# A decode kernel whose VectorE instructions leave the hardware loop and are written out in line

## The chip, the cores and the metric

The kernel runs on one core of one Trainium2 chip. The time is the device time of one execution in microseconds; "before" stands for the median of three runs. A profile is one further execution, recorded by the hardware profiler.

## The reference

One token (x, 1024 wide) goes through an attention block with a long cache and, beside it, through a small MLP mixer. Cut to what matters:

```python
xn = layernorm(x)
# A: attention, 32 query heads, 4 key/value heads, 65536 cached positions of 128
q = (layernorm-ed x @ wq) -> 32 heads of 128
scores = q . k_cache * 128 ** -0.5
o = softmax(scores) @ v_cache
A = o @ wo
# B: mixer
h  = gelu(layernorm(xn) @ w1)
x1 = xn + shifted(h) @ w2
B  = x1 + gelu(layernorm(x1) @ w3) @ w4
out = x + A + B
```

K and V together are 128 MiB of bfloat16, each element of which is used once; wq, wo and the four MLP weights are another 34 MiB.

## The kernel before

The kernel is written without a scheduler. Each engine has a recorder (class `_Q`, line 14): `wait`, `op` and `dma` append to a list of operations, and what an operation must wait for is worked out from buffers that note who wrote and read them last (`_deps`, line 119). At the end (lines 700 to 704) each list is emitted to its engine. `emit` (line 64) writes the list out in line. `emit_looped` (line 67) needs marks in the list: it checks that the stretches between marks have the same shape, and that every semaphore value grows by the same step from stretch to stretch, then emits one stretch as the body of a hardware loop. In the loop a wait's value is computed by register instructions (line 56, `i * steps[k] + ...`), and the loop ends in a register operation, a compare and a branch (line 93). Before the change VectorE (`q_dve`) and TensorE (`q_pe`) are emitted as loops; SyncE, ScalarE and GpSimd are written out.

The attention is 32 tiles (`NT`): 4 heads of 8 tiles, a tile being 8192 positions. The loop at line 584 records the tiles; every fourth tile is a mark, so that a loop body holds 4 tiles and runs 8 times. For tile n:

- `Ttr` (line 484): VectorE transposes K in 4 pieces of 128x1024 (L490) from the load buffer into a second buffer. The pieces of tile n+1 stand between the steps of tile n. They are what frees a K buffer.
- `QK` (line 493): 16 matmuls of PE into `S_ps` (L500).
- `stats1`, `MB`, `stats2`: the row maximum on VectorE (L509), its spread (L510), a small matmul (L515) and a reduction (L519).
- `EXP` (line 522): the running bound on VectorE (L528), ScalarE's exponential (L530), the change of the bound on VectorE (L532) and its exponential (L534).
- `PTr` and `PV` (lines 536 and 542): the weights are transposed by PE (L538) and VectorE (L540), then 16 matmuls with V (L548). They are what frees a V buffer.
- `FLASH` (line 553): ScalarE copies the result out (L556), GpSimd scales and adds it (L558 to L561).

SyncE issues all the large loads in one queue. K and V come in loads of 4 MiB, two tiles each, into two buffers of each kind; the load two steps ahead is recorded after the tile that frees its buffer (line 603). Weights follow in the same queue: w1 and w2 after tile 28, w3 after tile 30 (L323 by way of `load_at`), wo and the first 16 of w4's 28 row groups after tile 31 (channel `w40`, landing in a buffer that is not used before), and three further parts of w4 (`w41` to `w43`) once w1 and w2 have been read.

Behind the tiles come the mixer (lines 618 to 643), the merging of the heads (667 to 677), w3 (679), and the last products, in an order written by hand: wo, then w4's first two parts by `half_rows` (L660, in pairs of matmuls, 64 for wo and 44 for w4), a copy by VectorE (L689), w4's third part by `out_rows` (L452), the fold of the copy (L691), w4's fourth part, the last copy (L696) and the store of the output.

Ahead of the tiles, VectorE has 42 operations of layer norms, constants and the query, then the 4 transposes of tile 0.

Of the kernel before, what the change touches and what calls it, by code (L numbers as in the profile page):

```python
# [172 lines left out]
def bass_parallel_sum__gqa_block_cached__mixer_s_mlp__decode_kernel(  # L173
# [31 lines left out]
    with ExitStack() as es:  # L205
# [8 lines left out]
        def sem(name):  # L214
            return E(nc.semaphore(name))
# [68 lines left out]
        q_pe = _Q("pe", sem("c_pe"), in_order=True)  # L284
        q_dve = _Q("dve", sem("c_dve"))
# [152 lines left out]
        def head_switch(h):  # L438

            _deps(q_pool, [b_Y], [b_Yc])  # L440
            src = Yall[:, (h - 1) % HKV, :, :, :]
            q_pool.ops.append((2, lambda e: e.tensor_copy(Ycur[:, :, :, :], src), s_y, 2))
            for b in (b_brun[1],):
                for s, v in list(b.w.items()) + list(b.r.items()):
                    q_pool.wait((s, v))
            q_pool.ops.append((2, lambda e: e.memset(brun[:, 1:2], BIG), s_b, 2))
# [37 lines left out]
        def Ttr(n, idx):  # L484

            s, half, xs = (n // 2) % 2, n % 2, n % 2
            for ix in idx:
                c = KOFF[s] // 2 + 4096 * half + 1024 * ix
                x = (XOFF + 8192 * xs) // 2 + 1024 * ix
                _op(q_dve, lambda e, c=c, x=x: e.transpose(out=KV32[:, x:x + 1024], in_=KV32[:, c:c + 1024]),  # L490
                    reads=[b_K[s][half]], writes=[b_X[xs][ix]])

        def QK(n):
            xs = n % 2
            fns = []
            for we in range(4):
                w_hi, e_ = divmod(we, 2)
                for cm in range(4):
                    mv = bass.AP(KV[:].tensor, XOFF + xs * 8192 + cm * 128 + w_hi * 64 + e_, [[kstep, P], [512, 16], [2, 32]])
                    fns.append(lambda e, we=we, cm=cm, mv=mv: e.matmul(  # L500
                        S_ps[32 * cm:32 * cm + 32, :], Ycur[:, we, :, :].rearrange("p a g -> p (a g)"), mv,
                        start=(we == 0), stop=(we == 3), tile_position=(0, 32 * cm)))
            if n % 4 == 0:
                q_pe.wait((s_y, n // 4 + 1))
            b_Yc.add_read(_grp(q_pe, fns, reads=b_X[xs], writes=[b_S]))

        def stats1(n):
            m = n % 2
            _op(q_dve, lambda e: e.reduce_max(mrow[:, m:m + 1], S_ps[:, :], axis=AX.X), reads=[b_S], writes=[b_mrow[m]])  # L509
            _op(q_dve, lambda e: e.tensor_tensor(out=Rm[:, m, :], in0=sel16[:, :], in1=mrow[:, m:m + 1].broadcast_to([P, 16]), op=ALU.mult),  # L510
                reads=[b_mrow[m], b_const], writes=[b_R[m]])

        def MB(n):
            m = n % 2
            _op(q_pe, lambda e: e.matmul(MB_ps[:, 0:16], Lmat[:, :], Rm[:, m, :], start=True, stop=True),  # L515
                reads=[b_R[m], b_const], writes=[b_MB])

        def stats2(n):
            _op(q_dve, lambda e: e.tensor_reduce(out=Bst[:, n % 4:n % 4 + 1], in_=MB_ps[:, 0:16], axis=AX.X, op=ALU.min),  # L519
                reads=[b_MB], writes=[b_Bcol[n % 4]])  # L520

        def EXP(n):
            m = n % 2
            ko = 1 - m
            cL = 513 * m
            if n % 4 == 0:
                q_dve.wait((s_b, n // 4 + 1))
            _op(q_dve, lambda e: e.tensor_tensor(out=brun[:, m:m + 1], in0=brun[:, ko:ko + 1], in1=Bst[:, n % 4:n % 4 + 1], op=ALU.min),  # L528
                reads=[b_brun[ko], b_Bcol[n % 4]], writes=[b_brun[m]])
            _op(q_act, lambda e: e.activation(p_sb[:, m, :], S_ps[:, :], ACTF.Exp, bias=brun[:, m:m + 1], scale=SCALE, accum_out=tmpO[:, cL:cL + 1]),  # L530
                reads=[b_S, b_brun[m]], writes=[b_p[m], b_tmpL[m]])
            _op(q_dve, lambda e: e.tensor_tensor(out=dd[:, m:m + 1], in0=brun[:, m:m + 1], in1=brun[:, ko:ko + 1], op=ALU.subtract),  # L532
                reads=[b_brun[ko], b_brun[m]], writes=[b_dd[m]])
            _op(q_act, lambda e: e.activation(ff[:, m:m + 1], dd[:, m:m + 1], ACTF.Exp), reads=[b_dd[m]], writes=[b_ff[m]])  # L534

        def PTr(n):
            m = n % 2
            _op(q_pe, lambda e: e.matmul(PT_ps[:, :], permR[:, :], p_sb[:, m, :], start=True, stop=True),  # L538
                reads=[b_p[m], b_const], writes=[b_PT])
            _op(q_dve, lambda e: e.transpose(out=pT_f[:, :], in_=PT_ps[:, :]), reads=[b_PT], writes=[b_pT])  # L540

        def PV(n):
            s = (n // 2) % 2
            v0 = VOFF[s] + 8192 * (n % 2)
            fns = []
            for q in range(16):
                q4 = q % 4
                fns.append(lambda e, q=q, q4=q4: e.matmul(OT_ps[32 * q4:32 * q4 + 32, :], pT_bf[:, q, :, 1],  # L548
                                                          KV[:, v0 + 512 * q:v0 + 512 * (q + 1)],
                                                          start=(q < 4), stop=(q >= 12), tile_position=(0, 32 * q4)))  # L550
            _grp(q_pe, fns, reads=[b_pT, b_V[s]], writes=[b_OT])

        def FLASH(n):

            m = n % 2
            _op(q_act, lambda e: e.activation(tmpO[:, 1:513], OT_ps[:, :], ACTF.Copy), reads=[b_OT], writes=[b_tmpO])  # L556
            _deps(q_pool, [b_ff[m]], [b_Oacc])
            q_pool.op(lambda e: e.tensor_tensor(out=spare[:, 4:5], in0=ff[:, m:m + 1], in1=ff[:, m:m + 1], op=ALU.add), False)  # L558
            b_Oacc.set_write(q_pool.op(lambda e: e.tensor_scalar(out=O_acc[:, :], in0=O_acc[:, :], scalar1=ff[:, m:m + 1], scalar2=0.0, op0=ALU.mult, op1=ALU.add)))  # L559
            _deps(q_pool, [b_tmpO, b_tmpL[m], b_Oacc], [])  # L560
            ev = q_pool.op(lambda e: e.tensor_tensor(out=O_acc[:, m:m + 513], in0=O_acc[:, m:m + 513], in1=tmpO[:, m:m + 513], op=ALU.add), tick=(s_fl, n + 5))  # L561
            _done(ev, [b_ff[m], b_tmpO, b_tmpL[m]], [b_Oacc])
# [15 lines left out]
        def load_at(c0, bufs, ch, w, r0, nrow):  # L578
            load_rows(KV[:, c0:c0 + nrow * w.shape[1]], bufs, ch, w, r0, nrow)
# [3 lines left out]
        const_sems = (q_pool.sem,)  # L583
        for n in range(NT):
            if n % 4 == 0:
                q_pe.mark(const_sems)
                q_dve.mark(const_sems)
            QK(n)
            Ttr(n + 1, [0])
            stats1(n)  # L590
            MB(n)
            stats2(n)
            EXP(n)
            Ttr(n + 1, [1])
            PTr(n)
            Ttr(n + 1, [2, 3])
            if n % NSUB == NSUB - 1:
                head_switch(n // NSUB + 1)
            PV(n)
            FLASH(n)  # L600
            if n % NSUB == NSUB - 1:
                head_end(n // NSUB)
            (issue_v if n % 2 else issue_k)(n // 2 + 2)
            if n == NT - 4:
                load_at(KOFF[0], b_K[0][:1], "k0", B_w1, 0, 8)
                load_at(KOFF[0] + 8192, b_K[0][1:], "w2", B_w2, 0, 8)
            if n == NT - 2:
                b_w3 = b_K[1] + [b_V[0]]
                load_at(VOFF[0], b_w3, "w3", B_w3, 0, 8)
            if n == NT - 1:  # L610
                b_wo = [b_V[1]] + b_X[0] + b_X[1]
                load_at(VOFF[1], b_wo[:1], "wo0", A_wo, 0, 16)
                load_at(XOFF, b_wo[1:], "wo1", A_wo, 16, 16)
                load_at(WOFF, [b_W], "w40", B_w4, 0, 16)
        for q in (q_pe, q_dve):
            q.mark(const_sems)

        _grp(q_pe, [lambda e, j=j, q=q: e.matmul(M0_ps[32 * q:32 * q + 32, :], xn2_bf[:, j:j + 1].broadcast_to([P, 32]),
                                                 KV[:, j * D + 512 * q:j * D + 512 * (q + 1)],
# [80 lines left out]
        q_sp.emit(nc.sync)  # L700
        q_act.emit(nc.scalar)
        q_pool.emit(nc.gpsimd)
        q_dve.emit_looped(nc, nc.vector)
        q_pe.emit_looped(nc, nc.tensor)


# [26 lines left out]
```

## Time and profile before

| | |
|---|---|
| median of 3 runs | 403.39 us (403.23 to 403.68) |
| profiled execution, its own time | 403.03 us |
| its span, first to last instruction | 401.7 us |
| mean granted TensorE clock | 0.63 |
| busy: PE, PE weight loads, VectorE | 183.4, 53.0, 238.8 us |
| busy: ScalarE, GpSimd | 49.7, 91.9 us |
| read from HBM | 169.87 MB, 423 GB/s over the span |
| transposes of K on VectorE (L490) | 132, 156.4 us busy, 1216 ns each |
| maxima on VectorE (L509), transposes of the weights (L540) | 32 of 675 ns, 32 of 713 ns |
| instructions in VectorE's program: before, after | 168, 469 |

A busy time is the sum of an engine's operations; register, branch and wait instructions are not counted in it. A wait is put down to what ended last before the waiting operation started. The DMA row of the page gives, for 40 equal slices of the span, the busy share of the core's 16 DMA engines in tenths. The trace further holds each DMA packet with queue, start, duration and size, and the events by which a load reports: 16 for each load.

### The profile page before, as it was taken

The page shows a single profiled execution, that of the slowest core. Times are in us where ns is not written, and L with a number is a line of the kernel's source. Part 1 is how long each engine was busy: PE and PEld are TensorE (multiplying, and loading weights), DVE is VectorE, ACT ScalarE, POOL GpSimd, SP SyncE. Part 2 cuts the span into 40 slices and gives each one's busy share as a digit, 9 for nine tenths or more (in the row PEclk, how much of TensorE's full clock was granted, in tenths as well). Part 3 has the DMA queues.
Part 4 walks back from the last instruction along what each step waited for, and adds up shares of the span by engine and source line. Part 5 has one row for each costly group of instructions (what it writes and reads, how often), then busy time and mean ns, then how long its engine had stood idle before and what let it go on. Part 6 is the DMA issues. An engine that isn't in the chain of part 4 may idle for free.

```text
span 401.7 us, 4258 instructions
## 1 busy us (share of the span) xinstructions
PE 183.4 (46%) x1428; PEld 53.0 (13%) x1428; DVE 238.8 (59%) x403; ACT 49.7 (12%) x132; POOL 91.9 (23%) x173
## 2 busy tenths in 40 slices
PE   0044245563545444443444443545453636636457
PEld 0022111110111111110111111111010101213112
DVE  0024788767575758585767585858585858664201
ACT  1000021211111111111112021111111112100000
POOL 6000022231315222222432221216222222430000
PEclk9997565555655556557565565565565565575988
DMA  9989999999999999999999999999999999999995
GB/s 392 444 365 441 444 417 418 457 423 425 434 437 431 422 437 431 431 424 450 424 431 431 437 431 424 434 434 428 424 454 421 431 424 427 456 410 424 429 419 212
DMA packets 6209, 169.98 MB, mean 423 GB/s; under 512 B 820, under 2 KB 824, under 8 KB 952
## 3 DMA queue, kind: packets, MB, share of 16 engines
q1 hardware_dynamic: 6056, 169.87, 98.5%
q8 instruction: 4, 0.07, 0.1%
q14 instruction: 5, 0.04, 0.0%
q10 hardware_dynamic: 144, 0.00, 0.0%
HBM read 169.87 MB, written 0.00 MB: 423 GB/s over the span
## 4 chain that ended last, share of the span: by engine, by line
DMA 56%; DVE 19%; issue 11%; PE 11%; ACT 1%; POOL 0%; DVEq 0%; SPq 0%; ACTq 0%; POOLq 0%
DMA KV<-in_A_k_cache_dram 40%; DVE KV L490 12%; DMA KV<-in_B_w_dram 10%; DMA x_bf<-in_A_x_dram 6%; PE S_ps L500 5%; DVE mrow L509 3%; PE PT_ps L538 2%; PE S_ps L660 2%; ACT p_sb L530 1%; PE MB_ps L515 1%; DVE Rm L510 1%; DVE Bst L519 1%; DVE brun L528 1%; DVE pT_f L540 1%; PE OT_ps L548 0%
## 5 line engine op out<-in xcount | busy, mean ns | idle before, releaser
L490 DVE STREAM_TRANSPOSE KV<-KV 128x1024 f32<-128x1024 f32 x132 | 156.4, 1216 | 52.8 <-DMA KV<-in_A_k_cache_dram 52.8
L548 PE MATMUL OT_ps<-KV,pT_f 128*32 128x512 bf16 x512 | 60.7, 627 | 26.6 <-DVE pT_f L540 26.6
L500 PE MATMUL S_ps<-KV,Ycur 128*32 128x512 bf16 x512 | 58.7, 606 | 16.9 <-DVE KV L490 16.9
L561 POOL TENSOR_TENSOR O_acc<-O_acc,tmpO 128x513 f32<-128x513 f32 x32 | 41.0, 1281 | 96.4 <-ACT tmpO L556 96.4
L530 ACT ACTIVATE p_sb<-S_ps,brun 128x512 bf16<-128x512 f32 x32 | 22.0, 687 | 162.4 <-DVE brun L528 162.4
L515 PE MATMUL MB_ps<-Rm,Lmat 128*128 128x16 bf16 x32 | 6.2, 192 | 74.6 <-DVE Rm L510 74.6
L538 PE MATMUL PT_ps<-p_sb,permR 128*128 128x512 bf16 x32 | 18.3, 571 | 45.9 <-ACT p_sb L530 45.9
L556 ACT ACTIVATE tmpO<-OT_ps 128x512 f32<-128x512 f32 x32 | 19.2, 599 | 106.1 <-PE OT_ps L548 106.1
L558 POOL TENSOR_TENSOR spare<-ff 128x1 f32<-128x1 f32 x32 | 6.2, 193 | 110.9 <-ACT ff L534 110.9
L509 DVE TENSOR_REDUCE mrow<-S_ps 128x1 f32<-128x512 f32 x32 | 21.6, 675 | 16.1 <-PE S_ps L500 16.1
L540 DVE STREAM_TRANSPOSE pT_f<-PT_ps 128x512 f32<-128x512 f32 x32 | 22.8, 713 | 2.9
L500 PEld LDWEIGHTS S_ps<-KV,Ycur 128*32 128x32 bf16 x512 | 14.7, 125 | 62.1 <-issue 32.4
L548 PEld LDWEIGHTS OT_ps<-KV,pT_f 128*32 128x32 bf16 x512 | 14.7, 129 | 58.6 <-DVE pT_f L540 30.7
L559 POOL TENSOR_SCALAR O_acc<-O_acc,ff 128x514 f32<-128x514 f32 x32 | 22.4, 700 | 0.0
L515 PEld LDWEIGHTS MB_ps<-Rm,Lmat 128*128 128x128 bf16 x32 | 3.3, 102 | 101.6 <-DVE Rm L510 101.6
L689 DVE COPY KV<-S_ps 64x512 f32<-64x512 f32 x1 | 0.7, 683 | 22.7 <-PE S_ps L660 22.7
L381 PE MATMUL MM_ps<-ln_s,ones_f 128*128 128x1 f32 x6 | 1.8, 362 | 27.2 <-DVE ln_s L380 27.2
L377 DVE CAST xT<-x_bf 128x8 f32<-128x8 bf16 x1 | 0.2, 171 | 21.5 <-DMA x_bf<-in_A_x_dram 21.5
L660 PE MATMUL S_ps<-KV,o_bf 128*1 128x512 bf16 x64 | 8.6, 429 | 5.7 <-DMA KV<-in_A_wo_dram 5.7
L519 DVE TENSOR_REDUCE Bst<-MB_ps 128x1 f32<-128x16 f32 x32 | 5.6, 175 | 9.2 <-PE MB_ps L515 9.2
L393 POOL TENSOR_TENSOR ln_s<-ln_s,neghalf 128x1 f32<-128x1 f32 x3 | 1.7, 558 | 40.3 <-DVE ln_s L391 40.3
L538 PEld LDWEIGHTS PT_ps<-p_sb,permR 128*128 128x128 bf16 x32 | 3.3, 103 | 48.7 <-ACT p_sb L530 48.7
(116 smaller groups left out, 128.2 us busy)
## 6 DMA issues: line engine op xcount, KB each, us to landing
KV<-in_A_k_cache_dram SPq DMA_DIRECT2D x16, 4096.0 KB, 23.3
KV<-in_A_v_cache_dram SPq DMA_DIRECT2D x16, 4096.0 KB, 22.0
KV<-in_A_wo_dram SPq DMA_DIRECT2D x2, 4096.0 KB, 27.5
KV<-in_B_w_dram SPq DMA_DIRECT2D x1, 7168.0 KB, 20.9
KV<-in_B_w_dram SPq DMA_DIRECT2D x2, 2048.0 KB, 24.9
KV<-in_B_w_dram SPq DMA_DIRECT2D x1, 4096.0 KB, 41.5
KV<-in_B_w_dram SPq DMA_DIRECT2D x1, 1536.0 KB, 41.8
KV<-in_B_w_dram SPq DMA_DIRECT2D x1, 1024.0 KB, 43.9
```

The source lines that it names most:

```text
L490: _op(q_dve, lambda e, c=c, x=x: e.transpose(out=KV32[:, x:x + 1024], in_=KV32[:, c:c + 1024]), reads=[b_K[s][half]], writes=[b_X[xs][ix]])
L500: fns.append(lambda e, we=we, cm=cm, mv=mv: e.matmul(S_ps[32 * cm:32 * cm + 32, :], Ycur[:, we, :, :].rearrange("p a g -> p (a g)"), mv, s ...
L509: _op(q_dve, lambda e: e.reduce_max(mrow[:, m:m + 1], S_ps[:, :], axis=AX.X), reads=[b_S], writes=[b_mrow[m]])
L515: _op(q_pe, lambda e: e.matmul(MB_ps[:, 0:16], Lmat[:, :], Rm[:, m, :], start=True, stop=True), reads=[b_R[m], b_const], writes=[b_MB])
L530: _op(q_act, lambda e: e.activation(p_sb[:, m, :], S_ps[:, :], ACTF.Exp, bias=brun[:, m:m + 1], scale=SCALE, accum_out=tmpO[:, cL:cL + 1]) ...
L538: _op(q_pe, lambda e: e.matmul(PT_ps[:, :], permR[:, :], p_sb[:, m, :], start=True, stop=True), reads=[b_p[m], b_const], writes=[b_PT])
L540: _op(q_dve, lambda e: e.transpose(out=pT_f[:, :], in_=PT_ps[:, :]), reads=[b_PT], writes=[b_pT])
L548: fns.append(lambda e, q=q, q4=q4: e.matmul(OT_ps[32 * q4:32 * q4 + 32, :], pT_bf[:, q, :, 1], KV[:, v0 + 512 * q:v0 + 512 * (q + 1)], sta ...
L556: _op(q_act, lambda e: e.activation(tmpO[:, 1:513], OT_ps[:, :], ACTF.Copy), reads=[b_OT], writes=[b_tmpO])
L559: b_Oacc.set_write(q_pool.op(lambda e: e.tensor_scalar(out=O_acc[:, :], in0=O_acc[:, :], scalar1=ff[:, m:m + 1], scalar2=0.0, op0=ALU.mult ...
L561: ev = q_pool.op(lambda e: e.tensor_tensor(out=O_acc[:, m:m + 513], in0=O_acc[:, m:m + 513], in1=tmpO[:, m:m + 513], op=ALU.add), tick=(s_ ...
L660: _grp(q_pe, [lambda e, lhs=lhs, rhs=rhs, jj=jj: e.matmul(S_ps[32 * jj:32 * jj + 1, :], lhs, rhs[:, 512 * jj:512 * jj + 512], start=False, ...
```

## The change

VectorE is no longer marked and no longer emitted as a loop. Its 32 tiles are emitted one after the other with constant wait values. Two side effects follow from the code: at a mark the recorder forgets which semaphore values have been waited for, so that without marks some repeated waits go; and a wait is no longer carried by a register instruction, so that an operation with two waits is preceded by a wait instruction. The order of the operations on all engines stays as it was, and PE keeps its loop of 4 tiles.

```diff
         for n in range(NT):
             if n % 4 == 0:
                 q_pe.mark(const_sems)
-                q_dve.mark(const_sems)
             QK(n)
             Ttr(n + 1, [0])
             stats1(n)
...
-        for q in (q_pe, q_dve):
-            q.mark(const_sems)
+        q_pe.mark(const_sems)
...
         q_pool.emit(nc.gpsimd)
-        q_dve.emit_looped(nc, nc.vector)
+        q_dve.emit(nc.vector)
         q_pe.emit_looped(nc, nc.tensor)
```

## The prediction

> **What bounds the kernel now.** I read, in this order, the page's slices and queues, the waits, the chain that ended last, the granted clock by stretches, and the trace's records of single DMA packets and of the events that each load posts. The page first:
>
> ```profile
> DMA  9989999999999999999999999999999999999995
> ...
> q1 hardware_dynamic: 6056, 169.87, 98.5%
> q8 instruction: 4, 0.07, 0.1%
> q14 instruction: 5, 0.04, 0.0%
> ```
>
> The reader is to see that the DMA engines are full from end to end but for a dip in the third slice, before the tiles begin, and that two small queues carry instructions over the same 16 engines. 169.87 MB in the 395 us from the first packet (1.8 us) to the last weights (397 us) are 430 GB/s. VectorE, on the other hand, has time to spare (waits):
>
> ```profile
> DVE KV L490 <- DMA KV<-in_A_k_cache_dram: 52.8, 14, 4.4
> ```
>
> Once per pair of tiles it waits for K, 3.8 us on average. Then the end of the chain (start, duration, work):
>
> ```profile
> 349.73 41.46 DMA KV<-in_B_w_dram
> ...
> 391.23 6.52 PE S_ps L660 x44
> ...
> 397.84 0.69 DVE KV L689
> ...
> 399.56 0.42 DVE p_sb L696
> ```
>
> The first part of w4 (chan w40) is issued at 349.73, queues behind other loads, lands at 391.19, and from there PE, VectorE and the output follow without a pause. So the end is set by when the **slowest** DMA engine finishes w40: a load is complete only when all its 16 events are in. For w40 these came from 389.17 to 391.19, a spread of 2.02 us.
>
> That spread is where this change can bite. At the third load of K and V (51.90) it was 0.56 us; at the next (62.94) it was 1.89, and it stayed near 2.0. In between lie two instruction fetches. The packet records of all fetches inside the kernel (start us, us of the fetch, us of the 32 KB packet behind it on the same engine; that packet's neighbours take 1.215):
>
> ```
> DVE   54.78   8 KB  0.325  1.875      POOL  94.60  8 KB  0.315  1.568
> PE    57.31  16 KB  1.100  1.681      ACT  138.45  8 KB  0.315  1.594
> PE    80.56  16 KB  1.087  1.687      POOL 276.18  8 KB  0.309  1.567
> PE   374.64  16 KB  0.928  1.764      ACT  340.16  8 KB  0.309  (16 KB packet: 0.989 against 0.613)
> ```
>
> A fetch sets back its DMA engine by its own time plus what the next packet loses: 0.325 + 0.660 = 0.985 us for DVE's, 0.66 to 0.69 for the four of POOL and ACT, 1.48 to 1.57 for PE's. The engine never makes it up, as nothing is idle: in the events of the later loads one entry jumps by just that amount and stays (POOL's from 2.06 to 1.40 us ahead of the last, then to 0.76; ACT's from 1.91 to 1.24, then 0.55). The assignment of owners is mine: at its two fetches ACT had run 65 and 190 rows, POOL 68 and 193, so each fetches once in 125 instructions; DVE had run 70 at 54.78 and its loop of 78 then fits what it holds. DVE's engine, by the jump from 1.63 to 0.65 ahead at 62.94, stands 0.84 us ahead of the last through the middle and 1.01 ahead at w40.
>
> **The change, part by part.**
>
> *Removed:* VectorE's register and branch work.
>
> ```profile
> L56 DVEq ALU_OP  x264: 40/40/52, 42.4 to 344.8; - x132
> ```
>
> With the loop's own rows these are 272 register operations of 40 ns (10.9 us), 24 fused ones of 46 (1.2) and 8 branches of 56 (0.5): 12.6 us. *Added:* 61 wait instructions, as two-semaphore waits of the straight code need one each; VectorE's four of before took 21 ns: 1.3 us. Most register rows lie under the preceding operation (the one at 133.02 runs inside L510, 133.01 to 133.18), so the gain of VectorE's chain is between 0 and 11.3 us, 0.35 per tile; I take 0.1 per tile. At the end it is worth **nothing**: the cover is the DMA queue. By issues against packets done, each load of K or V finds 2.5 MiB (6.0 us) to 5.2 MiB (12.5 us) still outstanding, the least at 55.34. The tightest place is w3, issued at 340.97 behind VectorE's transposes with 1.0 MiB left. Its first packet ran at 342.41; the latest DMA engine only finished the load before it at 344.46, so 2 us of delay there are free, and an earlier issue gives no time. If that cover were gone, a gain of at most 0.35 us per tile would show.
>
> About two wait instructions per tile are added, mostly before L528 and L532; behind them on VectorE stand the transposes of the next tile, and ACT's exponential waits for L528: 21 ns each, in the place of a 40 ns register row. No DMA is moved, SP's and POOL's orders are the same, and PE's loop is untouched.
>
> *Added, and on the path:* code. VectorE's program grows from 168 to 469 instructions. At one fetch per 125, with the first at row 70, fetches fall at rows 70, 195, 320 and 445: tile 2 (65 us), tile 12 (160), tile 22 (257) and the layer norm behind the tiles (L383, about 360 us). The first replaces the one of before. **Three more land on DVE's DMA engine before w40 is complete.** Each costs between 0.66 (POOL, ACT) and 0.985 us (DVE's own). I take 0.67, as four of the five 8 KB rows have it, and keep the other end. Ahead of the last by 1.01, minus 3 x 0.67, makes this engine the last one by **1.0 us**; with 0.985 by 1.95. The lateness shows from tile 23 on (0.5) and all of it at w40 to w43. A w3 issued 0.5 us later is inside the 2 us named.
>
> The Trainium skill, "Runtime: NRT & Kernel Launch", section "Instruction fetch mechanics", holds that straight code is streamed ahead in 16 KiB blocks whose crossing is mostly hidden, and that it is branches that cost; by it this change would be free or a small gain, 403.4 or less. The trace agrees that no engine stops at its fetches, differs in the size (8,192-byte packets here, except PE's), and shows the hidden fetch paid for by the data on that DMA engine.
>
> *The tail.* How much of 1.0 us reaches the end depends on PE's granted clock (columns: stretch, PE, weight loads, DVE, ACT, POOL, clock, DMA share, GB/s):
>
> ```profile
> 391.06:394.47 3.41, 3.24 (x16) 1.01 (x18) 0.00 (x0) 0.00 (x0) 0.00 (x0) 0.50 0.99 419
> 394.47:397.89 3.42, 3.42 (x45) 1.55 (x42) 0.05 (x1) 0.00 (x0) 0.00 (x0) 1.00 0.67 273
> ```
>
> The 44 matmuls go in 22 pairs: 0.427 us a pair at clock 0.50, 0.213 at 1.00. If the step at 394.47 stays where it is, a start at 392.23 does 5.3 pairs slowly and 16.7 fast and ends 0.5 us later instead of 1.0; w43, landing at 399.60 in place of 398.60, then lets the last L452 start at 399.64 instead of 399.11, also 0.53. If the step moves with the start, all 1.0 arrives. PE will have been idle 5.8 us instead of 4.8 before w40, which speaks for a slow start, so I lean to the upper end: **+0.9**. The rest of the chain (L689, L691, L696, output) is as before.
>
> Sum: the profiled execution took 403.03 (span 401.70 and 1.33 around it); 403.03 + 0.9 = 403.93. It lies 0.36 below the median of the three runs shown, 403.39; carried to the median, **404.3 us**. A measurement of this kernel can tell about 0.2%, 0.8 us.
>
> **Rivals.**
>
> *The fetches miss the late engine.* For: the owners are inferred, and 12 of 16 DMA engines are 1.5 to 2.0 us ahead at most loads; three fetches of 0.67 on one of those, 2.0 in all, only draw level. It also holds if only two more fetches come before w40 (lead 1.01, minus 1.34: 0.33 late). This decides from a lead of 2.0 us. Against: the jump of 0.985 to 0.65 ahead fits no other fetch. Time: +0 to +0.35, 403.4 to 403.7, not slower.
>
> *Each fetch costs what DVE's own did.* For: it is the only row of that queue's owner. Against: four others agree on 0.67. The lateness is 1.95, of which the fixed clock step passes 1.5 (first pair at 393.19: 3 slow, 19 fast; w43 at 400.55) and the moving one all: 404.9 to 405.3.
>
> *VectorE stops at a block that has not come.* A fetch takes its turn behind a packet of 1.2 us and then 0.3. A stop of 1.5 us is inside every cover above; over 2 us at tiles 28 to 31 it starves the late engines at w3, and adds the excess, up to 1 us: 405.3 or more. Against: with about 100 us between fetches the block is asked for long before it is used; ACT and POOL show no gap there.
>
> *The leaner VectorE reaches the end.* Only if a load now waits for DMA work to be issued; none of the late engines does. At most 0.35 us for each of the last two tiles: 402.7.
>
> **How the numbers follow.** Forecast case (1.0 late, +0.5 to +1.0: 403.9 to 404.4) 0.50; DVE's own price 0.25; missing the late engine 0.17; VectorE stopping 0.04; reaching the end 0.04. Slower by over 0.2%, that is over 404.2: 0.6 of the forecast case, all of the second and the fourth: 0.30 + 0.25 + 0.04 = 0.59. Faster: 0.04. Within 0.2%: 0.37. The range goes from 403.5 (part of the missing case) to 405.3 (the dearer fetch).
>
> **What would show it.** Right: four 8 KB fetches more or less evenly spaced by 125 rows of VectorE beside the four of ACT and POOL, eight in place of five; from about 267 us the loads' last events 0.5 us late, w40's 1.0 late (near 392.2), with one event alone behind the rest; VectorE's wait for K no shorter at the end. Wrong: w40 at 391.2 with eight fetches (another DMA engine), fewer fetches, a gap on VectorE at a fetch, or a DMA engine idle before w3.

## The result, and the profile after

The changed kernel takes 405.67 us (median of 7 runs, 404.77 to 406.25) against 403.23 for the kernel before (median of 7 runs beside it). The ratio is 1.0054, 95% interval 1.0041 to 1.0067: slower by 2.2 us (1.65 to 2.7). The profiled execution, the fastest of the seven, took 404.77 us with a span of 403.5, after 403.03 and 401.7.

The page of the changed kernel, DMA slices and instruction queues:

```profile
DMA  9989999999999999999999999999999999999994
...
q8 instruction: 4, 0.07, 0.1%
q14 instruction: 8, 0.07, 0.0%
```

The DMA engines are as full as before, and three instruction fetches have come in, five to eight. Two of VectorE's waits (total, times, longest):

```profile
DVE KV L490 <- DMA KV<-in_A_k_cache_dram: 56.8, 14, 5.1
...
DVE pT_f L540 <- PE PT_ps L538: 6.3, 28, 0.2
```

VectorE waits 4.0 us longer for K in all. Of that, 0.85 is an earlier start of the tiles in this execution (first transpose at 41.39, before 42.24) and 1.3 is K itself coming later (VectorE goes on with the last load of K at 326.73, before 325.42). What is left, 1.8 us or 0.06 per tile, is what its chain has gained. The second line is new: at the transpose of the weights VectorE is now 0.22 us ahead of PE and waits for it. The end of the chain of waits, in order of time (start, duration, work):

```profile
350.77 42.50 DMA KV<-in_B_w_dram
...
393.32 6.27 PE S_ps L658 x42
...
399.68 0.69 DVE KV L687
...
401.40 0.42 DVE p_sb L694
```

It is the same chain (two source lines earlier by the diff); PE starts on w40 at 393.32 in place of 391.23. From there to the end the two kernels hardly differ. So the time came in before w40 landed, and the packet records and the loads' events say where:

```
VectorE's fetches (start us; fetch, next 32 KB packet):
   53.75 0.325 1.875    157.93 0.325 1.875    263.34 0.334 1.875    362.69 0.325 1.867
last event of the load, before -> after (us):
   131.13 -> 131.30    160.27 -> 160.59    267.13 -> 268.43    361.86 -> 364.19    w40 391.19 -> 393.27
last three events of the load, us to the last one, after:
   150.73  -0.83 -0.44 0     160.59  -0.59 -0.16 0     268.43  -1.59 -1.14 0     w40  -2.11 -1.22 0
```

An engine that was 0.83 us ahead of the last becomes the last at the second fetch, 0.16 behind the former one; the third and the fourth put it 0.98 further back each. At w40, 15 DMA engines have been done for 1.2 us when the sixteenth comes in.

One place is less full than the DMA row shows. As K comes late, VectorE frees w3's place late: w3 is issued at 342.10 in place of 340.97, and its first packet runs at 343.06 in place of 342.41. By the packet records, 12.1 of the 16 engines are busy on average between 342 and 343 us, where it was 15.8 before. These are the engines that were ahead. The two latest ones ended the load before w3 at 345.06 and 346.22 by its events, so they had work throughout, and w40 did not suffer.

### The profile page after: what moved, and what is told of

It reads as the page before. It is cut to its first block, busy times and chain, and to the rows that moved or that the text cites. A ratio compares the mean times of both kernels' runs of the same rounds, so it can differ in the third digit from the quotient of the medians.

```text
span 403.5 us, 4014 instructions
## 1 busy us (share of the span) xinstructions
PE 185.0 (46%) x1428; PEld 52.9 (13%) x1428; DVE 239.4 (59%) x403; ACT 49.8 (12%) x132; POOL 91.7 (23%) x173
## 4 chain that ended last, share of the span: by engine, by line
DMA 57%; DVE 23%; PE 11%; issue 6%; ACT 1%; POOL 0%; SPq 0%; ACTq 0%; DVEq 0%; POOLq 0%
DMA KV<-in_A_k_cache_dram 41%; DVE KV L490 14%; DMA KV<-in_B_w_dram 11%; DMA x_bf<-in_A_x_dram 6%; PE S_ps L500 5%; DVE pT_f L540 3%; DVE mrow L509 3%; PE PT_ps L538 2%; PE S_ps L658 2%; ACT p_sb L530 1%; PE MB_ps L515 1%; DVE Rm L510 1%; DVE Bst L519 1%; DVE brun L528 1%; PE OT_ps L548 0%
## 5 line engine op out<-in xcount | busy, mean ns | idle before, releaser
L658 PE MATMUL S_ps<-KV,o_bf 128*1 128x512 bf16 x64 | 10.0, 482 | 6.1 <-DMA KV<-in_A_wo_dram 6.1
```

Source lines behind the costliest of these rows:

```text
L658: _grp(q_pe, [lambda e, lhs=lhs, rhs=rhs, jj=jj: e.matmul(S_ps[32 * jj:32 * jj + 1, :], lhs, rhs[:, 512 * jj:512 * jj + 512], start=False, ...
```

## The experiments

| kernel | VectorE's program | w40 lands | ratio to before (interval) |
|---|---|---|---|
| before | 168 | 391.19 | |
| changed | 469 | 393.27 | 1.0054 (1.0041 to 1.0067) |
| e1 loop, 375 waits ahead | 543 | 402.93 | 1.0288 (1.0271 to 1.0305) |
| e7 loop, 360 waits in two places | 528 | 393.16 | 1.0059 (1.0042 to 1.0077) |
| e2 loop, 375 waits on ScalarE | 168 | 392.56 | 1.0043 (1.0027 to 1.0059) |
| e4 last 8 tiles written out | 266 | 391.37 | 1.0000 (0.9989 to 1.0011) |
| e3 last 16 written out | 362 | 392.16 | 1.0021 (1.0011 to 1.0032) |
| e6 last 20 written out | 410 | 392.01 | 1.0025 (1.0012 to 1.0037) |
| e5 all, and 125 waits | 594 | 394.28 | 1.0070 (1.0056 to 1.0084) |
| e8 all, and PE written out | 469 | 392.93 | 1.0045 (1.0029 to 1.0061) |
| e9 before, PE kept awake | 168 | 391.84 | 0.9965 (0.9953 to 0.9977) |
| e10 changed, PE kept awake | 469 | 393.19 | 1.0018 (1.0006 to 1.0029) |

The theory: code is what costs; each 8 KB of it is fetched through one DMA engine, and that engine's part of every later load is late. The rival: the written-out tiles themselves cost, through their waits and their pace on VectorE.

**e1 and e7: the loop stays, code is added.**

```diff
# e1, on the kernel before: behind its first instruction, 375 instructions of two satisfied waits each
+        q_dve.ops += [(0, q_dve.sem, 1)] * 750
# e7: 350 in that place, and behind the last gelu:
+        q_dve.ops += [(0, q_dve.sem, 1)] * 370
```

> The kernel before (VectorE still in its loop), with 375 wait instructions on VectorE ahead of everything, on a semaphore that is long satisfied, in the 22 us in which VectorE waits for x. VectorE's program is then 543 instructions long, its tiles are as before. Theory (code length: each 8 KB of VectorE's program is fetched through one DMA engine and sets it back by 0.98 us for good): four VectorE fetches in place of one, all in the first 25 us; VectorE's DMA engine is the last at every K and V load of the middle, w40 lands 2.0 us later than before (about 393.2), time +2.0 us. Rival (the written-out tiles themselves are what costs: their waits, their pace on VectorE): tiles are looped here, so w40 at 391.2 and time +0.

The run is spoilt by its own waits, which took 38 us. VectorE's waits in it, and the DMA row of its page:

```profile
DVE xT L378 <- issue: 37.9, 1, 37.9
```

```profile
DMA  9999981999999999999999999999999999999995
```

VectorE reads x at 39.4 in place of 22.9, the tiles start 16 us later, more than the queue holds, and the seventh slice shows the DMA engines idle. The time tells nothing between the two theories. The loads' events show one thing more: VectorE's first three fetches set one event 2.6 us behind all others (load landing at 54.43, spread 3.09), and behind the idle stretch the spread is 0.65 (landing at 83.54). Here the dry queue wiped the lateness out.

> The kernel before (VectorE still in its loop), with 175 satisfied wait instructions on VectorE in its wait for x and 185 more in its wait for the last products, behind L478. In the first try 375 of them took 38 us, 0.10 us each, and outlasted the wait for x; 17.5 us and 18.5 us now stay inside 21.5 and 22.7. VectorE's program is 528 instructions long. Theory: fetches at rows 70, 195, 320 and 445 (about 3, 16, 360 and 386 us), three more than before at 0.98 us: 2.95 - 1.01 = 1.9 us late at w40, near 393.1, time +1.9 us. Rival (the written-out tiles are what costs): w40 at 391.2, time +0.

Measured: one fetch at 12.46, among 64 KB packets (2.96 behind it, neighbours 2.42), and VectorE's fetches in the 32 KB stretches at 27.89, 361.59 and 390.49, each with a packet of 1.87 behind it; w40 at 393.16 (393.1 expected), ratio 1.0059. The loop is that of the kernel before and the loss is that of the changed kernel. **The rival falls.**

**e2: the same on ScalarE.** The same line with `q_act`, behind the issue of x.

> The kernel before, with 375 satisfied wait instructions on ScalarE behind its issue of the load of x, in the 30 us in which it waits for the query's product. VectorE's program is as before. Theory: five ScalarE fetches in place of two, at 0.69 us each on ScalarE's DMA engine, which stood 0.72 us ahead of the last at w40: 3 x 0.69 - 0.72 = 1.35 us late; w40 near 392.5, time +1.35 us. Rival (something in VectorE's straight code, not code fetches): +0.

Measured: w40 at 392.56, ratio 1.0043, 1.7 us (1.1 to 2.4). Another engine's code costs as VectorE's does, at its own price: its packets behind a fetch took 1.593 to 1.596.

**e3, e4, e6: how much is written out.** The marks of VectorE end at tile 16 (24, 12), and what follows is in line:

```diff
-                q_dve.mark(const_sems)
+                if n <= 16:
+                    q_dve.mark(const_sems)
```

> The first 16 tiles of VectorE in the loop (4 passes), the last 16 written out: 362 instructions. Theory: fetches at rows 70, 195 and 320, two more than before, of 0.98 us: 1.96 - 1.01 = 0.95 us late; w40 near 392.15, time +0.95 us. Rival (a cost per written-out tile, 2.2 us over 32): +1.1 us by its price, without w40 having to land late by one event alone.

> The first 24 tiles of VectorE in the loop (6 passes), the last 8 written out: 266 instructions. Theory: fetches at rows 70 and 195, one more than before: 0.98 - 1.01 = level with the last DMA engine; w40 at 391.2 and time +0 to +0.1 us, although a quarter of the tiles is written out. Rival (a cost per written-out tile): +0.55 us.

> The first 12 tiles of VectorE in the loop (3 passes), the last 20 written out: 410 instructions. Theory: the cost goes by whole fetches, and 410 instructions need no more of them than the 362 with 16 tiles in the loop: rows 70, 195 and 320, the next would be 445. w40 near 392.15, time +0.95 us, the same as there. Rival (a cost per written-out tile): 2.2 x 20 / 32 = +1.4 us, 0.3 more than with 16 in the loop.

Measured: w40 at 392.16, 391.37 and 392.01; ratios 1.0021, 1.0000, 1.0025. e4 writes out a quarter of the tiles for nothing: its second fetch (320.68) uses up the lead of VectorE's DMA engine. That lead was only 0.47 us in this execution, so the engine became the last by 0.50; then PE's fetch at 376.03, which every version has, put another engine level with it. At w40 two events are last there, 0.02 us apart. e3 and e6 need the same three fetches, with 48 instructions between them, and in both the event of VectorE's engine is the last at w40, by 1.12 and 0.39 us. In time alone e3 and e6 do not separate the theories (the rival's 1.1 and 1.4 us lie in their intervals); e4 does, just (0.55 us against 0.44 at the upper end), and the count of fetches and the last event do.

A landing in the table is that of one execution, and landings of the same loads scatter. Up to wo, e9 below runs the code of the kernel before, and w40 lands 0.65 later in it: PE's fetch at 375.30 put its engine 0.89 behind the one that had been last, where it was 0.17 in the profile of before. So a difference of a few tenths between two landings tells nothing by itself.

**e5: more code on top.** The line of e1 with 250 waits, 125 instructions, in the changed kernel.

> The changed kernel with 125 satisfied wait instructions more on VectorE, ahead of everything, in its wait for x: 594 instructions. Theory: five VectorE fetches instead of four; the DMA engine that is already the last gets 0.98 us later, all of it reaches w40: near 394.25, time +3.1 us against the kernel before (+0.98 against the changed one). Rival (the written-out tiles cost, not their fetches): +2.2 us as for the changed kernel.

Measured: a fifth fetch, w40 at 394.28 (394.25 expected), ratio 1.0070, 2.8 us (2.3 to 3.4). The rival's 2.2 lies just below that interval.

**e8: PE written out as well.** `q_pe.emit(nc.tensor)` in the last line of the changed kernel.

> The changed kernel with PE written out too: some 950 recorded operations more on PE, about twice that in rows of the trace, so seven to eight more 16 KB fetches by PE at 1.56 us each. Theory: what counts is on which DMA engines they fall. The three fetches of PE in the kernel before fell on three different ones. If each falls on another engine, w40 is set by the worse of VectorE's engine and of one that is hit once or twice: w40 393.3 to 395, time +2.2 to +4 against the kernel before. If they take turns on three or four engines, two or three more on each: +3 to +5 us late beyond PE's three of before, w40 395 to 396. Rival (code fetches don't matter, PE's branches cost): time at or below that of the changed kernel, +2.2 or less.

The instruction queues of its page:

```profile
q8 instruction: 11, 0.18, 0.2%
q14 instruction: 8, 0.07, 0.0%
```

Measured: seven PE fetches more, w40 at 392.93, a little under what was expected, ratio 1.0045, 1.8 us (1.2 to 2.5), which is under the expected 2.2 to 4 and is what the rival says. VectorE's DMA engine alone is still the last, the next one 0.72 us ahead. In the loads' events PE's first eight fetches each move another entry by 1.56; the last three (334.94, 370.59, 388.91) move entries that seem to have moved once before. That fits PE's fetches going round about eight DMA engines, a reading of the entries' sizes, since the trace does not name the engine. Spread like this they cost the end nothing here. By time alone this run does not tell the theory from its rival.

**e9 and e10: what the tail does with a late landing.** In every profile so far PE ran at half clock behind w40. The changed kernel, three stretches of granted clock (columns as in the prediction):

```profile
389.23:392.65 3.42, 0.75 (x8) 0.09 (x4) 0.00 (x0) 0.00 (x0) 0.00 (x0) 1.00 0.87 369
392.65:396.06 3.41, 2.74 (x14) 0.86 (x16) 0.00 (x0) 0.00 (x0) 0.00 (x0) 0.50 0.97 408
396.06:399.47 3.41, 3.41 (x32) 1.19 (x28) 0.00 (x0) 0.00 (x0) 0.00 (x0) 1.00 0.44 178
```

The step to full clock, at 394.47 in the kernel before, is at 396.06 here: it moved 1.6 us with a landing that moved 2.1. That it followed the landing is not shown: in each profile all changes of the clock lie on one grid of 3.41 us, and the grid lies elsewhere in each execution (steps at 391.06 before, 392.65 here, 392.11 in e4). In e7 the half clock held for two stretches:

```profile
391.54:394.95 3.41, 1.75 (x10) 0.57 (x12) 0.00 (x0) 0.00 (x0) 0.00 (x0) 0.50 0.96 404
394.95:398.36 3.41, 3.41 (x20) 1.05 (x18) 0.00 (x0) 0.00 (x0) 0.00 (x0) 0.50 0.59 240
398.36:401.78 3.42, 2.98 (x46) 1.19 (x42) 0.68 (x1) 0.00 (x0) 0.00 (x0) 1.00 0.05 17
```

There the way from w40 to the end took 11.5 us, in the changed kernel 10.2. (In e1 to e4 the half clock held for one stretch, in e5 to e8 for two.) So PE was kept at work in its wait, in both kernels:

```diff
+        _grp(q_pe, [lambda e: e.matmul(PT_ps[:, :], permR[:, :], wo_sb[:, 0:512],
+                                       start=True, stop=True)] * 20, reads=[b_const], writes=[b_PT])
         half_rows(*w4_rows(0))
```

> The kernel before, with 20 matmuls of 128x512 more on PE between wo and the first part of w4, into a bank that nothing reads (they add nothing to the output), to keep PE busy in its 4.8 us of waiting for w40. Theory for the tail: what of the landing's lateness reaches the end is decided by PE's clock, 0.50 for 3.2 us or more behind w40 in every profile so far. Awake, PE does the 22 pairs in 4.7 us, is done by 396 to 397, and the end hangs on w43 alone (398.6 in the profile of before): 0.5 us earlier than its profiled execution, 1 to 1.5 earlier than executions in which the half clock lasts two stretches; time -0.5 to -1.0 us against before. Forty rows more also bring PE's fourth fetch forward from 398.3 into the landing of w41 to w43, on a DMA engine that is ahead. Rival (the tail is bound by its own chain whatever the clock): +0, or up to +1 where the added matmuls run at half clock past 391.

> The changed kernel with the same 20 matmuls. Theory: w40 to w43 land 2.0 us later than in the kernel before, PE is awake, the end hangs on w43 alone (400.7 in the profile of the changed kernel): 0.3 to 1.5 us less than the changed kernel, so +0.7 to +1.9 against before, and 2.0 more than the same matmuls cost or gain in the kernel before. Rival: the difference between the two with an awake PE is smaller than 1 us, and part of what the change cost was PE's clock rather than the landing.

e9, the stretches and the end of the chain:

```profile
387.82:391.24 3.42, 3.26 (x20) 1.38 (x16) 0.00 (x0) 0.00 (x0) 0.00 (x0) 1.00 0.85 364
391.24:394.65 3.41, 3.41 (x27) 1.30 (x26) 0.00 (x0) 0.00 (x0) 0.00 (x0) 1.00 0.99 416
```

```profile
353.55 44.46 DMA KV<-in_B_w_dram
...
398.05 0.61 PE OUT_ps L452 x16
...
398.67 0.61 PE OUT_ps L692 x8
...
399.30 0.42 PE OUT_ps L452 x8
```

PE stays at full clock, and the chain now goes through w4's third part, which lands at 398.00; the fourth part lands at 399.26, just as PE gets to it (399.30). In this profile the end follows the DMA engines. Measured: 402.46 us (402.05 to 403.12), ratio 0.9965, 1.4 us (0.9 to 1.9) less than before, with 0.5 to 1.0 expected: this version beats both kernels. The changed kernel with the same matmuls takes 404.37 (404.11 to 404.54), ratio 1.0018. Between the two lie 1.9 us. With PE's clock out of the way the change costs about what it costs with it; the rival of e10 falls. Both spread less than without the matmuls (0.4 us over 12 runs in e10, against 1.5 over 7 in the changed kernel; 1.1 over 9 in e9, against 2.5 over 20 in the kernel before).

## Why the prediction was wrong

**Where it was right.** What bounds the kernel (the slowest DMA engine's part of w40); that VectorE's leaner code is worth nothing at the end (0.1 us per tile taken, 0.06 measured); the number of fetches, three more before w40, and their places (160, 257 and 360 us expected; 157.9, 263.3 and 362.7), while the first came at 53.75 in place of 65; no stop of VectorE. The lead of VectorE's DMA engine (0.84 us in the middle, 0.83 measured) agreed in part by luck: read from the jump at its next fetch, it was 0.63 in e10, 0.47 in e4 and 0.86 in e6.

**A sign of being wrong that did show.** "A DMA engine idle before w3" was to show the prediction wrong. Engines were idle there, the ones that were ahead, and it came from the same late K, not from a stop of VectorE. The cover of 2 us was worked out for the latest engine alone, and for that one it held.

**The step that failed is a price.** "Each costs between 0.66 (POOL, ACT) and 0.985 us (DVE's own). I take 0.67, as four of the five 8 KB rows have it": VectorE's own row was the one to take, and the prediction had no reason but the count for taking the others. Every one of its fetches measured among 32 KB packets, in the changed kernel and in e2 to e8, has a packet of 1.87 behind it: 0.98 us. With 3 x 0.98 less the lead of 1.01 the engine is 1.94 us late, where the prediction had 1.0; w40 came 2.08 later (the head of that execution was 0.13 later on its own).

**A second term was a little too small.** The tail was given "+0.5 to +1.0" out of 1.0, with a lean to the upper end, since the clock step might have stayed where it was. It neither stays nor is it shown to move with the start: it lies on a grid whose place differs from execution to execution, so one profile could not price it. Over the runs time follows w40: 0.18 us later gives 0.0, 0.8 to 1.0 give 0.85 to 1.0, 1.4 gives 1.7, 1.7 gives 1.8, 2.0 to 2.1 give 2.2 to 2.4, 3.1 gives 2.8, each with an interval of about half a microsecond and a landing from one execution. Within that, all of a late landing reaches the end. The forecast was +0.9 and 2.2 came: of the 1.3 us between them 0.94 is the price, and the rest is no larger than the interval.

**The rivals.** "Each fetch costs what DVE's own did" was the true case, with a chance of 0.25 and 404.9 to 405.3; the measured median lies above its range and above the range as a whole, but its loss of 1.5 to 1.95 us reaches into the interval of the ratio (1.65 to 2.7). The other three did not happen. "Missing the late engine" is nearly what e4 shows when there is one fetch more instead of three.

**What stays open.** Why a packet behind VectorE's fetch loses 0.66 us, behind ScalarE's 0.38 and behind GpSimd's 0.35, at the same 8 KB. It went with the engine whose code is fetched in all runs; no run here tells the cause.

## What to carry to other kernels

Where every load waits for its slowest DMA engine and the queue never runs dry, ask of each change what it puts on single DMA engines: instruction fetches are 0.1% of the bytes, and here each of VectorE's costs up to 1 us at the end. Written-out code was free here up to the next block and as long as its DMA engine had a lead (e4). Read the lead from the spread of a load's events, in more than one execution, and the price from the same engine's own fetch, not from a majority of others. Behind a last load, keeping a waiting PE at full clock was worth 1.4 us here (e9), more than half of what the change cost.

## What the runs showed of the hardware

A wait instruction on two satisfied semaphores, 21 to 50 ns in the trace, took 0.10 us of VectorE's time when 375 stood in a row. By the loads' events the fetches of VectorE, ScalarE and GpSimd each stayed on one DMA engine, those of PE fit a round of about eight. PE's half clock behind a wait of 3.3 to 4.8 us came in stretches of 3.41 or 6.83 us whose places differ from execution to execution; the way from w40 to the end took 10.2 to 11.8 us with it, and 10.0 to 10.1 with PE kept awake.
